# Entering the feed-forward steps: the second batch's A tiles in Bz buffers, their transfers ahead of later reads, and Bs asked for a unit earlier

## The chip, the cores and the metric

The kernel runs on one core of a Trainium2 chip. The metric is the device time of one execution in microseconds; the median of several executions counts. Beside it there is a profiled execution with its trace.

## The reference

Eight batches of 3008 x 256 (float32) go through a Fourier layer and then through a feed-forward network:

```python
X = np.fft.rfft(x, axis=1)
Yr = Xr @ w_r - Xi @ w_i + b_r;  Yi = Xr @ w_i + Xi @ w_r + b_i
Yr, Yi = soft_threshold(Yr, 0.01), soft_threshold(Yi, 0.01)
y = np.fft.irfft(Yr + 1j * Yi, n=3008, axis=1)          # -> 24064 x 256
h = y @ moe_w_in                                        # 256 -> 2048
g = np.where(h > 0, h, np.exp(np.minimum(h, 0)) - 1)    # ELU
out = g @ moe_w_out                                     # 2048 -> 256, float32
```

## The kernel before

**Fourier part, in units.** 3008 is split into 47 x 64, and each transform is two small matrix products with a trip through DRAM between them. A batch is worked in units: six A units (`unit_A`, first forward product from the x tiles `xt`; casts into an A tile, which is stored to the DRAM buffer DA), a load of Z from DA (`load_Z`, in two parts), eight X units (second forward product, into XT), twelve M half units (the complex weights, bias and soft threshold, into Y), six B units (`unit_B`, first inverse product, into a Bz tile, stored to the DRAM buffer DB), four loads of Bs from DB (`load_Bs`), and eight Y units (`unit_Y`, second inverse product, into yT). Two Y units share one Bs tile.

**Feed-forward part, in steps.** A step works one pair of 128-wide slices of the hidden dimension for 512 tokens: `front` multiplies yT with w_in_s into the PSUM tile hps and takes its exponential on ScalarE into Et; `elu` limits Et ("E" in the prediction); `finish_elu`, called in the next step, combines Et and hps into gT; and `back`, two steps behind (`LAG = 2`), multiplies gT with w_out_r into ps_o. Eight steps make a block of 512 tokens, after which ps_o is copied to osb and stored ("outs"). There are 47 steps to a batch. hps has two PSUM buffers, so step i+2 needs the gT of step i. A step without a unit is "free" and may take the exponential in halves and have GpSimd do the limiting.

**Order.** The order of the instructions on each engine is written out by hand. In the opening the first batch goes through all of its units alone; then come the second batch's six A units and the first batch's first two Y units, with matmuls on constants between them (`idle_pe(n)`, n matmuls whose result is dropped). From then on `plan` lays the units of the following batches over the steps, one to a step: `f0` runs before a step's `front`, `f1` after `finish_elu`. `lead` shifts the first batch's list by some steps.

**Queues.** Stores and most loads are issued by SyncE (SP), in program order; x and w_out are loaded from GpSimd's queue. w_out comes in two halves; the second holds the slices from ps_o 4 on, the fifth `back`. A `gate` is a copy of one element on GpSimd: it holds that queue back until a load has landed. w_in comes in four quarters, each scaled into w_in_s when it is there (`scale_w_in`); the last is scaled in two pieces on VectorE (DVE) in steps 3 and 4 and first used in step 6.

**Buffers.** Tiles with one tag share buffers in turn. The second batch's A tiles 1 and 2 lie in the buffers of the tag gT (three), which the steps then need.

The tail of the opening, as it is before:

```python
    for u in range(6):
        unit_A(1, u, on_dve=bool(u % 2), ahead=True)
        if u == 1:
            scale_w_in(1, True)
            for w in (2, 3):
                load_Bs(0, w)
            gate(Bs_of[0, 2][:, 0, 0:1])
            load_w_out(1)
            load_w_in(3)
        idle_pe(2)
    scale_w_in(2, False)
    for s0, s1 in ((0, 8), (8, NS)):
        load_Z(1, s0, s1)
    idle_pe(3)
```

Of the kernel before, what the change touches and what calls it, by code (L numbers as in the profile page):

```python
# [8 lines left out]
ALU = mybir.AluOpType  # L9
AF = mybir.ActivationFunctionType  # L10
BF16 = mybir.dt.bfloat16
# [18 lines left out]
def kernel(  # L30
# [11 lines left out]
    nc = tc.nc  # L42
    P = nc.NUM_PARTITIONS

    B, S, D = x.shape
# [33 lines left out]
    wk2 = ctx.enter_context(tc.tile_pool(name="wk2", bufs=2))  # L79
# [19 lines left out]
    A_of = {}  # L99
# [6 lines left out]
    Bs_of = {}  # L106
# [22 lines left out]
    def unit_A(b, u, alone=False, on_dve=False, ahead=False):  # L129
        ci, uu = u // 2, u % 2  # L130
        if uu == 0:
            if ahead and ci > 0:
                A_of[b, ci] = late3.tile([P, 8, D], BF16, name="A", tag="gT")
            elif alone:
                A_of[b, ci] = wk4.tile([P, 8, D], BF16, name="A", tag="Bs")
            else:
                A_of[b, ci] = wk2.tile([P, 8, D], BF16, name="A", tag="A")
            if ci == 0:
                DA_of[b] = dram.tile([NJ, P, D], BF16, name="DA", tag="DA")
        xt, A = xts[ci], A_of[b, ci]  # L140
        dav = DA_of[b].rearrange("j p d -> p j d")
        ps = unit_ps("aps", alone or ahead)
        for j in range(2):
            nc.tensor.matmul(  # L144
                ps[:, j, :], lhsT=M1[:],
                rhs=xt[:, 4 * uu + 2 * j : 4 * uu + 2 * j + 2, :], start=True, stop=True,
            )
        evac(
            A[:, 4 * uu : 4 * uu + 4, :].rearrange("p n d -> p (n d)"),
            ps[:].rearrange("p a b -> p (a b)"), on_dve,  # L150
        )
        j0 = 8 * ci
        if alone:
            j0 += 4 * uu
            nc.sync.dma_start(dav[:, j0 : j0 + 4, :], A[:, 4 * uu : 4 * uu + 4, :])
        elif uu == 1:
            nc.sync.dma_start(dav[:, j0 : j0 + 8, :], A[:])
# [109 lines left out]
    def load_Bs(b, w):  # L267

        Bs = wk4.tile([4 * K1, 8, D], BF16, name="Bs", tag="Bs")
        dv = DB_of[b].rearrange("k (c h m) d -> (k c h) m d", c=2, h=2)  # L270
        nc.sync.dma_start(Bs[:], dv[:, 8 * w : 8 * w + 8, :])
        Bs_of[b, w] = Bs

    def unit_Y(b, u, alone=False, on_dve=False):
        w, dt = u // 2, u % 2
        if u == 0:
            yT_of[b] = late2.tile([P, 2, S], BF16, name="yT", tag="yT")
        yT, Bs = yT_of[b], Bs_of[b, w]
        ps = unit_ps("yps", alone)
        psv = ps[:].rearrange("p a (k j) -> p (a k) j", j=P)  # L280
        for j in range(8):
            nc.tensor.matmul(  # L282
                psv[:, j, 0 : 2 * N1], lhsT=Bs[:, j, dt * P : dt * P + P], rhs=M4[:],
                start=True, stop=True,
            )
        evac(
            yT[:, dt, w * WT : w * WT + WT].rearrange("p (r j) -> p r j", j=8),
            psv[:, :, 0 : 2 * N1].rearrange("p j r -> p r j"), on_dve,
        )
# [5 lines left out]
    def idle_pe(n):  # L295

        for _ in range(n):
            nc.tensor.matmul(ips[:], lhsT=busy[:, 0:P], rhs=busy[:], start=True, stop=True)
# [274 lines left out]
    def load_w_in(q):  # L573
        if q < 3:
            wf = late3.tile([P, 2, FQ], F32, name="w_in_f", tag="Et")
        else:
            wf = late2.tile([P, 2, FQ], F32, name="w_in_f", tag="osb")
        nc.sync.dma_start(wf[:], w_in_v[:, :, q * FQ : q * FQ + FQ])
        w_in_f.append(wf)

    def load_w_out(hh):
        hf = slice(hh * NFT // 2, (hh + 1) * NFT // 2)
        nc.gpsimd.dma_start(w_out_r[:, hf, :], w_out_v[:, hf, :])

    def gate(src):

        t = gatep.tile([P, 1], F32, name="gate", tag="gate")
        nc.gpsimd.tensor_copy(t[0 : src.shape[0], :], src)
# [66 lines left out]
    def scale_w_in(q, on_dve, c=slice(0, 2)):  # L655
        dst = w_in_s[:, c, q * FQ : q * FQ + FQ]
        if on_dve:
            nc.vector.tensor_scalar_mul(dst, w_in_f[q][:, c], 2.0 / S)
        else:
            nc.scalar.activation(dst, w_in_f[q][:, c], AF.Copy, scale=2.0 / S)  # L660

    scale_w_in(0, True)
    for u in range(6):
        unit_A(1, u, on_dve=bool(u % 2), ahead=True)
        if u == 1:
            scale_w_in(1, True)
            for w in (2, 3):
                load_Bs(0, w)
            gate(Bs_of[0, 2][:, 0, 0:1])
            load_w_out(1)  # L670
            load_w_in(3)
        idle_pe(2)
    scale_w_in(2, False)
    for s0, s1 in ((0, 8), (8, NS)):
        load_Z(1, s0, s1)
    idle_pe(3)
    for u in range(2):
        unit_Y(0, u, alone=True, on_dve=bool(u % 2))
    first.close()

    psF = ctx.enter_context(
# [61 lines left out]
            g_of[i] = gT  # L743
        late_elu.clear()

    def elu(i, hps, Et, on_pool, on_act):

        E_ = Et[:]
        if on_pool:
            for s in range(2):  # L750
                eng = nc.vector if i == n - 1 and s == 0 else nc.gpsimd
                eng.tensor_scalar(E_[:, s], E_[:, s], 1.0, 0.0, ALU.min, ALU.max)  # L752
        elif not on_act:
            nc.vector.tensor_scalar(E_, E_, 1.0, -1.0, ALU.min, ALU.add)  # L754
        late_elu.append((i, hps, Et, on_pool or on_act, on_pool))

    def back(i, split):
        blk, fp = divmod(i, NPAIR)
# [41 lines left out]
    def plan(b):  # L800

        f0 = [[] for _ in range(PER)]
        f1 = [[] for _ in range(PER)]
        n1, n2 = b + 1, b + 2
        mid = [("X", u) for u in range(8)] + [
            ("M", 0, 0), ("M", 0, 1), ("M", 1, 0), ("M", 1, 1), ("B", 0), ("M", 2, 0),
            ("M", 2, 1), ("B", 1), ("M", 3, 0), ("M", 3, 1), ("B", 2), ("M", 4, 0),
            ("M", 4, 1), ("B", 3), ("M", 5, 0), ("M", 5, 1), ("B", 4),
            ("A", 0), ("B", 5), ("A", 1), ("A", 2), ("A", 3), ("A", 4),
        ]  # L810
        if n1 < B:
            lead, seq = int(b == 0), [("y", u) for u in range(2, 6)] + mid
            seq.insert(20 if b else 4, ("y", 6))
            seq.insert(24 if b else 5, ("y", 7))
            xs = (3, 8, 13)
            seq += [("A", 5), ("n", 0), ("n", 1)] if b else [("n", 0), ("n", 1), ("A", 5)]
        else:
            lead, seq = 0, [("y", u) for u in range(2, 8)]
        for t, u in enumerate(seq, lead):
            if u[0] == "y":  # L820
                f0[t].append(put("Y", b, u[1]))
            elif u[0] == "n":
                f0[t].append(put("Y", n1, u[1]))
            elif u[0] == "A":
                if n2 < B:
                    f0[t].append(put("A", n2, u[1]))
            else:
                f0[t].append(put(u[0], n1, *u[1:]))
            if u == ("A", 1):
                f1[t] += [(load_Bs, (n1, w)) for w in range(4)]  # L830
            if u == ("A", 5) and n2 < B:
                f1[t] += [(load_Z, (n2, s0, s1)) for s0, s1 in ((0, 8), (8, NS))]
        if b == 0:
            f1[3].append((scale_w_in, (3, True, 0)))
            f1[4].append((scale_w_in, (3, True, 1)))
            f1[xs[0]].append((lambda: gate(Z_of[1][:, 16, 0:1]), ()))
        if n2 < B:
            for ci in range(3):
                f1[xs[ci]].append((load_x, (n2, ci)))
        return f0, f1  # L840
# [3 lines left out]
    for i in range(n + LAG):  # L844
        if i < n:
            r = i % PER
            if r == 0:
                f0, f1 = plan(i // PER)
                used = [bool(u0 or u1) for u0, u1 in zip(f0, f1)]
            free = not used[r]  # L850
            bare = bare + 1 if free else 0
            calm = free and (i >= n - 2 or (r + 2 < PER and not used[r + 1] and not used[r + 2]))
            for f, a in f0[r]:
                f(*a)
            on_act = any(f is unit_M for f, a in f0[r])
            h = front(i, calm and bare % 3 == 1, on_act, free and i > 0)
        finish_elu()
        if i < n:
            for f, a in f1[r]:
                f(*a)  # L860
            split = i > LAG and (i - LAG) % NPAIR == NPAIR - 1
            if split:
                back(i - LAG, True)
            elu(i, *h, free and i > 0, on_act)
        else:
            split = False
        if i >= LAG and not split:
            back(i - LAG, False)
# [30 lines left out]
```

## Time and profile before

| what | value |
|---|---|
| median of 3 runs | 912.44 us (912.34 to 914.53) |
| profiled execution | 911.36 us, its span 909.6 us |
| granted TensorE clock over the span | 0.997 |
| TensorE (PE) busy | 893.2 us, 98% |
| VectorE (DVE) busy | 717.5 us, 79% |
| ScalarE (ACT) busy | 696.8 us, 77% |
| GpSimd (POOL) busy | 314.9 us, 35% |
| DMA | 106.24 MB, mean 117 GB/s |

The span runs from the first to the last instruction of the program; the execution's time is 1.8 us longer. Times inside the trace count from the span's start. PE is the matmuls, PEld the weight loads beside them; SPq is SyncE's queue of DMA issues. A number in brackets behind a row is the idle time of the engine before it and what ended it.

### The profile page before, as it was taken

To read this page: it belongs to the slowest core of one execution; us is meant where nothing else is said; L and a number is where in the kernel's file an instruction comes from. 1 tells how busy PE (TensorE), PEld (TensorE's weight loads), DVE (VectorE), ACT (ScalarE), POOL (GpSimd) and SP (SyncE) were. 2 spreads that over 40 slices of the span, in tenths; PEclk is the share of its full clock that TensorE was granted. 3 is DMA by queue.
4 is the path that set the end of the run, shared out by engine and by line. 5 is a ranking of instruction groups with operands and counts; after the bars stand their busy time and mean duration, and the time that the engine had idled before them with its cause. 6 is when DMAs were issued, how large, how long until landed. Compare 5 with 4: busy or idle time off the path is not lost.

```text
span 909.6 us, 17270 instructions
## 1 busy us (share of the span) xinstructions
PE 893.2 (98%) x6721; PEld 652.3 (72%) x6721; DVE 717.5 (79%) x891; ACT 696.8 (77%) x850; POOL 314.9 (35%) x438
## 2 busy tenths in 40 slices
PE   8989999999999999999999999999999999999997
PEld 3447667876688667886678766787667866777775
DVE  8669778887788778897788877888778877778776
ACT  6768788777878778787787888778887877767664
POOL 6701540333321441405404153033332134443664
PEclk9999999999999999999999999999999999999999
DMA  8997116721283215732166032752228111231011
GB/s 270 309 269 228 47 48 186 209 70 47 77 241 124 71 47 143 190 109 85 56 201 194 24 99 59 217 161 72 69 72 230 30 42 47 82 82 48 24 48 46
DMA packets 90670, 106.24 MB, mean 117 GB/s; under 512 B 5270, under 2 KB 81308, under 8 KB 87228
## 3 DMA queue, kind: packets, MB, share of 16 engines
q1 hardware_dynamic: 84332, 77.62, 30.6%
q0 software_dynamic: 5968, 27.26, 9.1%
q8 instruction: 52, 0.85, 0.4%
q10 hardware_dynamic: 288, 0.26, 0.1%
q14 instruction: 30, 0.25, 0.1%
HBM read 55.32 MB, written 49.81 MB: 116 GB/s over the span
## 4 chain that ended last, share of the span: by engine, by line
PE 85%; DVE 5%; ACT 3%; DMA 3%; issue 2%; POOL 1%; SPq 1%; DVEq 0%; ACTq 0%; POOLq 0%
PE ps_o L773 34%; PE hps L715 34%; PE mps L192 9%; PE yps L282 2%; PE bps L244 2%; PE xps L175 2%; PE aps L144 2%; DMA Bs<-DB 2%; DVE gT L742 1%; DVE Et L754 1%; ACT Et L729 1%; ACT Et L726 1%; DMA xt<-in_x_dram 1%; DVE osb L784 1%; ACT Bz L257 1%
## 5 line engine op out<-in xcount | busy, mean ns | idle before, releaser
L773 PE MATMUL ps_o<-w_out_r,gT 128*128 128x256 f32 x3008 | 477.0, 301 | 0.2 <-DVE gT L740 0.2
L773 PEld LDWEIGHTS ps_o<-w_out_r,gT 128*128 128x128 f32 x3008 | 403.4, 189 | 50.3 <-DVE osb L784 1.3
L715 PE MATMUL hps<-yT,w_in_s 128*128 128x512 bf16 (+4 forms) x1728 | 389.9, 353 | 2.5 <-DVE gT L742 1.2
L740 DVE SCALAR_TENSOR_TENSOR gT<-Et,hps 128x512 fp32r<-128x512 f32 (+1 forms) x272 | 222.8, 848 | 75.3 <-POOL Et L752 38.2
L742 DVE SCALAR_TENSOR_TENSOR gT<-hps,Et 128x1024 fp32r<-128x1024 f32 x198 | 242.2, 1223 | 16.5 <-PE ps_o L773 1.0
L715 PEld LDWEIGHTS <-w_in_s 128*128 128x128 bf16 x1728 | 141.6, 98 | 129.4 <-issue 23.0
L729 ACT ACTIVATE Et<-hps 128x1024 f32<-128x1024 f32 x198 | 204.0, 1030 | 13.2 <-PE hps L715 6.7
L752 POOL TENSOR_SCALAR Et<-Et 128x512 f32<-128x512 f32 x187 | 111.4, 615 | 222.9 <-ACT Et L724 222.9
L754 DVE TENSOR_SCALAR Et<-Et 128x1024 f32<-128x1024 f32 x198 | 137.0, 692 | 48.0 <-ACT Et L729 40.1
L210 POOL TENSOR_SCALAR clip<-yb 128x512 f32<-128x512 f32 x84 | 51.7, 615 | 316.0 <-DVE yb L202 278.6
L724 ACT ACTIVATE Et<-hps 128x512 f32<-128x512 f32 x188 | 102.1, 595 | 63.9 <-PE hps L715 63.9
L726 ACT ACTIVATE Et<-hps 128x1024 f32<-128x1024 f32 x84 | 86.3, 1027 | 71.5 <-PE hps L715 71.0
L211 POOL TENSOR_TENSOR Y<-yb,clip 128x512 bf16<-128x512 f32 x84 | 107.2, 1276 | 7.0
L727 ACT ACTIVATE Et<-Et 128x1024 f32<-128x1024 f32 x84 | 88.8, 1058 | 2.7
L202 DVE TENSOR_TENSOR yb<-mps,bias_bc 128x512 f32<-128x512 f32 x89 | 61.4, 689 | 35.4 <-PE mps L192 28.6
L127 ACT CAST XT<-xps 128x768 bf16<-128x768 f32 x61 | 48.8, 800 | 15.8 <-PE xps L175 15.8
L127 ACT CAST yT<-yps 128x752 bf16<-128x752 f32 x63 | 49.7, 788 | 14.2 <-PE yps L282 14.1
L192 PE MATMUL mps<-wcat_r,XT 128*128 128x512 bf16 x192 | 58.2, 384 | 0.8 <-ACT Bz L257 0.3
L127 ACT CAST A<-aps 128x1024 bf16<-128x1024 f32 x45 | 45.6, 1014 | 15.3 <-PE aps L144 13.8
L192 PE MATMUL mps<-wcat_s,XT 128*128 128x512 bf16 x192 | 57.1, 379 | 0.0
L192 PEld LDWEIGHTS <-XT 128*128 128x128 bf16 x384 | 30.8, 98 | 29.6 <-DVE XT L125 0.6
L257 ACT CAST Bz<-bps 128x1024 bf16<-128x1024 f32 x46 | 46.0, 1000 | 2.5 <-PE bps L244 2.5
(110 smaller groups left out, 412.9 us busy)
## 6 DMA issues: line engine op xcount, KB each, us to landing
xt<-in_x_dram POOLq DMA_DIRECT2D x21, 1024.0 KB, 7.1
out_dram<-osb SPq DMA_DIRECT2D x158, 128.0 KB
Bs<-DB SPq DMA_DIRECT2D x32, 384.0 KB
DA<-A SPq DMA_DIRECT2D x21, 512.0 KB
DB<-Bz SPq DMA_DIRECT2D x21, 512.0 KB
Z<-DA SPq DMA_DIRECT2D x7, 1152.0 KB
Z<-DA SPq DMA_DIRECT2D x11, 384.0 KB
xt<-in_x_dram POOLq DMA_DIRECT2D x6, 512.0 KB, 5.9
```

The lines of the kernel that those rows point to most:

```text
L127: nc.scalar.copy(dst, src)
L192: nc.tensor.matmul(ps, lhsT=XT[:, dt, c, o : o + P], rhs=wm[:, dt, :], start=(not biased and m == 0 and dt == 0), stop=(m == 1 and dt == 1),)
L211: nc.gpsimd.tensor_tensor(Y_of[b, q][:, i, :], yb, clip[:], ALU.subtract)
L715: nc.tensor.matmul(hps[:, s, c0:c1], lhsT=w_in_s[:, dt, ft * P : ft * P + P], rhs=yT_of[b][:, dt, t0 : t0 + c1 - c0], start=(dt == 0), sto ...
L724: nc.scalar.activation(E_[:, s], hps[:, s], AF.Exp)
L726: nc.scalar.activation(E_, hps[:], AF.Relu, scale=-1.0)
L729: nc.scalar.activation(E_, hps[:], AF.Exp)
L740: nc.vector.scalar_tensor_tensor(o, e, -1.0, h, ALU.add, ALU.max)
L742: nc.vector.scalar_tensor_tensor(o, h, 0.0, e, ALU.max, ALU.add)
L752: eng.tensor_scalar(E_[:, s], E_[:, s], 1.0, 0.0, ALU.min, ALU.max)
L754: nc.vector.tensor_scalar(E_, E_, 1.0, -1.0, ALU.min, ALU.add)
L773: nc.tensor.matmul(po[q][:, i_ % 2, :], lhsT=gT[:, s, i_ * P : i_ * P + P], rhs=w_out_r[:, ft, :], start=(ft == 0 and i_ % 2 == 0), stop=( ...
```

## The change

Six edits. In the opening, the second batch's A tiles 1 and 2 are given the buffers of the tag Bz. The loads of the first batch's last two Bs tiles, the gate, the second half of w_out and the last quarter of w_in are issued after all six A units, and so behind all three stores to DA, instead of after the second. The idle matmuls ahead of the first two Y units become seven instead of three, and two are added behind them. In the steps, the first batch's list begins at step 2 instead of 1. Steps 0 and 1, both free now, take the exponential, the limiting and the combining in halves, on ScalarE and VectorE. In every batch the four Bs tiles are asked for in the step of the last B unit instead of that of the second A unit, which comes one step later.

```diff
             if ahead and ci > 0:
-                A_of[b, ci] = late3.tile([P, 8, D], BF16, name="A", tag="gT")
+                A_of[b, ci] = wk2.tile([P, 8, D], BF16, name="Bz", tag="Bz")
...
         if u == 1:
             scale_w_in(1, True)
-            for w in (2, 3):
-                load_Bs(0, w)
-            gate(Bs_of[0, 2][:, 0, 0:1])
-            load_w_out(1)
-            load_w_in(3)
         idle_pe(2)
     scale_w_in(2, False)
+    for w in (2, 3):
+        load_Bs(0, w)
+    gate(Bs_of[0, 2][:, 0, 0:1])
+    load_w_out(1)
+    load_w_in(3)
     for s0, s1 in ((0, 8), (8, NS)):
         load_Z(1, s0, s1)
-    idle_pe(3)
+    idle_pe(7)
     for u in range(2):
         unit_Y(0, u, alone=True, on_dve=bool(u % 2))
+    idle_pe(2)
     first.close()
...
-    def elu(i, hps, Et, on_pool, on_act):
+    def elu(i, hps, Et, on_pool, on_act, halves):
...
         elif not on_act:
-            nc.vector.tensor_scalar(E_, E_, 1.0, -1.0, ALU.min, ALU.add)
-        late_elu.append((i, hps, Et, on_pool or on_act, on_pool))
+            for s in range(2) if halves else (slice(0, 2),):
+                nc.vector.tensor_scalar(E_[:, s], E_[:, s], 1.0, -1.0, ALU.min, ALU.add)
+        late_elu.append((i, hps, Et, on_pool or on_act, halves))
...
-            lead, seq = int(b == 0), [("y", u) for u in range(2, 6)] + mid
+            lead, seq = 2 * int(b == 0), [("y", u) for u in range(2, 6)] + mid
...
-            if u == ("A", 1):
+            if u == ("B", 5):
                 f1[t] += [(load_Bs, (n1, w)) for w in range(4)]
...
-            h = front(i, calm and bare % 3 == 1, on_act, free and i > 0)
+            h = front(i, calm and bare % 3 == 1, on_act, free)
...
-            elu(i, *h, free and i > 0, on_act)
+            elu(i, *h, free and i > 1, on_act, free)
```

## The prediction

> **What bounds the kernel now.** The page comes first. TensorE is busy for 98% of the span, so what a change can win or lose lies in TensorE's idle time and in matmuls at a lowered clock.
>
> ```profile
> span 909.6 us, 17270 instructions
> PE 893.2 (98%) x6721; PEld 652.3 (72%) x6721; DVE 717.5 (79%) x891; ACT 696.8 (77%) x850; POOL 314.9 (35%) x438
> ```
>
> The timeline of TensorE alone, 54 to 74 us, shows where the edited lines run: the entry from the opening into the feed-forward steps. "Step i" is iteration i of the main loop; hps i, gT i and ps_o i are its two products and what lies between.
>
> ```profile
> 55.16 0.84 PE L282 MATMUL yps<-M,Bs 96*128 96x94 bf16 x16 [1.01 <-DMA Bs<-DB]
> 56.54 1.55 PE L715 MATMUL hps<-yT,w_in_s 128*128 128x512 bf16 x4 [0.54 <-ACT yT L127]
> 58.51 1.91 PE L715 MATMUL hps<-yT,w_in_s 128*128 128x512 bf16 x4
> 64.53 1.02 PE L715 MATMUL hps<-yT,w_in_s 128*128 128x512 bf16 x4 [0.96 <-DVE gT L742]
> 71.65 1.28 PE L773 MATMUL ps_o<-w_out_r,gT 128*128 128x256 f32 x8
> ```
>
> The brackets are the idle time before a row. hps 1 takes 1.91 us where the settled form takes 1.02. The last row, at 71.65, is ps_o 4, the first to read the second half of w_out. Two other timelines (DVE, and POOL) show what stands before it:
>
> ```profile
> 63.25 1.23 DVE L742 SCALAR_TENSOR_TENSOR gT<-hps,Et 128x1024 fp32r<-128x1024 f32 x1 [1.04 <-PE ps_o L773]
> 59.37 0.55 POOL L588 CAST gate<-Bs 96x1 f32<-96x1 bf16 x1 [15.26 <-DMA Bs<-DB]
> 59.87 0.97 POOL L583 DMA_DIRECT2D w_out_r<-in_moe_w_out_dram  x1
> ```
>
> gT 1 waits 1.04 us for ps_o 0, since the A tiles hold two of the three gT buffers. The gate waits for the third Bs tile and only then is w_out asked for; the tile view of w_out_r gives 9.6 us from issue to landing, so it lands at 69.45: 2.2 us ahead of ps_o 4. The SyncE queue and the windows view (us in the window, busy times of PE, PEld, DVE, ACT, POOL, then granted clock, DMA share, GB/s):
>
> ```profile
> 52.47 1.54 SPq L271 DMA_DIRECT2D Bs<-DB  x2
> 54.05 1.55 SPq L578 DMA_DIRECT2D w_in_f<-in_moe_w_in_dram  x1
> 55.70 1.64 SPq L157 DMA_DIRECT2D DA<-A  x2
> 66.83 0.82 SPq L164 DMA_DIRECT2D Z<-DA  x2
> 61.00:66.00 5.00, 3.80 (x31) 2.86 (x30) 3.62 (x5) 3.38 (x5) 0.00 (x0) 1.00 1.23 345
> 66.00:74.00 8.00, 8.00 (x78) 6.31 (x77) 7.45 (x11) 6.74 (x8) 0.00 (x0) 1.00 1.03 262
> 74.00:77.00 3.00, 3.00 (x29) 2.58 (x27) 2.76 (x3) 2.62 (x4) 1.57 (x3) 1.00 0.00 0
> 54.04:57.45 3.41, 1.75 (x20) 1.03 (x20) 1.22 (x2) 0.79 (x1) 0.00 (x0) 1.00 1.05 323
> 57.45:60.87 3.42, 3.42 (x22) 2.01 (x21) 1.58 (x2) 2.11 (x3) 1.47 (x2) 0.50 1.03 267
> ```
>
> From 52 to 74 us the DMA engines never pause, and at 74 they fall to nothing: a solid train of 6.3 MB (four Bs 1.57 MB, three DA 1.57, w_in 0.52, w_out 1.05, Z 1.57). In such a train an order is a deadline. And a 3.41 us stretch in which TensorE was busy for 1.75 us was followed by one at half clock.
>
> Last, the chain of waits around the second batch's first Y unit:
>
> ```profile
> 143.24 6.07 DMA Bs<-DB
> 149.31 0.05 issue
> 149.35 0.51 PE yps L282 x8
> ```
>
> TensorE stands 0.91 us there, and 1.03 us at 796.8 in the last batch. Beyond 66 us those are its only gaps over 0.2 us.
>
> **The change part by part.** *Idle matmuls.* Six more at 0.216 us (five took 1.25 us, the last draining) are 1.3 us. Four lie in the 1.01 us wait for Bs, two in the 0.54 us wait for yT. Cost nothing; without that cover 1.3. They keep 54.04 to 57.45 busy, so hps 0 and 1 run at full clock.
>
> *Bz buffers, halves, Y a step later.* The Bz tiles' reads were asked for by 44.95 and the DMA engines were at 0 GB/s from 51 to 52, so the new A tiles wait for nothing (cost 0; a wait would show on the casts of 50 to 54 us). I redo the steps from their durations: hps 0.86 issued, ps_o 0.93, a Y unit 0.35, a whole exp 1.03, E 0.69, gT 1.23 (1.14 to the next start), halves 0.6, 0.4, 0.66. hps 0 is issued by 57.7 (it waits for yT until 57.03 as before), halved exps end at 59.0, gT 0 at 60.75 (before 61.21). hps 1 and Y 2 run to 58.9, then TensorE waits. hps 2 60.8 to 61.65, ps_o 0 to 62.6, Y 3 to 62.95; gT 1 has its own buffer and ends by 62.7; hps 3 to 63.8, ps_o 1 to 64.75, Y 4 to 65.1, hps 4 to 65.95, ps_o 2 and Y 5 to 67.25.
>
> *The train.* Bs 2 and 3, the gate, w_out's second half and w_in's last quarter move behind two DA transfers: 2 x 0.524 MB at 345 GB/s is 3.04 us. The gate goes from 59.37 to 62.4, w_out's issue to 62.9. Bs 2 lands at 62.3, before Y 4 at 64.75. w_in's last packet was at 61.5 by the packet records, so 64.5, landed near 65.5; DVE's scaling at step 3, in front of E 3, would be ready at 64.9 and waits 0.6 us. gT 3 then ends at 67.9, hps 5 to 68.8, ps_o 3 and Y 6 to 70.1, hps 6 (after gT 4 at 70.2) to 71.1. There ps_o 4 wants w_out. Before, the same point was 72.0 (71.65 is its early start) with Y 7 done, 0.35 us: with w_out in time the entry is 72.0 - 71.1 - 0.35 = 0.55 us shorter.
>
> w_out is not in time. Z waits for the last DA; that DA's packets now end at 60.1 (57.07 + 3.04), and before Z was issued 0.5 us after them: so at 60.7, ahead of w_out at 62.9. The bytes are the same, the train ends at 74.0 as before, but its last car is w_out where it was Z. From last packet to landing w_out took 0.95 us (68.5 to 69.45), and its last packets straggle: 75.2. ps_o 4 starts at 75.2 instead of 72.0, one Y unit behind: 3.2 + 0.35 = **+3.55 us**. Bounds: 69.7 (served on arrival: 1.1 us to the first packet, as the x load at 75.93, then 5.7 as before) and 76.0 (1 us of straggling).
>
> Why last: in the packet records a newcomer waits for what another queue already holds. The out stores issued at 80.04 send nothing until x's packets thin out at 84; the DB store issued at 36.82 nothing until 39.25, when w_out's first half thins out; w_out itself, issued at 59.87, nothing until 63.75. The Trainium skill, "DMA: Bandwidth & Descriptors", section on queues, rings and completion order, has each DMA engine go round robin between queues packet by packet; by equal turns w_out would pass Z, which is the first rival below. The trace shows such turns only from 64 to 65 us (about 50 packets each per quarter), after the wait.
>
> *Clock.* TensorE then idles from 71.1 to 75.2. A stretch busy for 1.75 of 3.41 us halved the next, so nearly wherever the stretches fall one follows. Half clock after the restart costs half of what is left of it: 0.85 to 2.5, I take **+1.5**. The Trainium skill, "TensorE: Matmul & The Clock Gate", Part 1, gives the slow state after at least one idle window of about 3.4 us; a 4.1 us gap holds a whole one in one phase of five, so by the page this term would mostly be 0 and the time 915.1. The row speaks for less idleness being enough.
>
> *Bs asked for earlier.* SyncE waits for the DB store to land; queued behind are A's stores, which nobody needs before Z is asked for. In the first batch outs now come just before that store, as they do in the last batch. From the start of B 5's matmuls: SP is done with four outs at 3.3 us (the outs of 139.87 began 0.6 into their step and took 2.6), DB lands 3.5 us later (789.86 to 793.35), Bs 4.4 after that (793.41 to 797.8): 11.2. The Y unit comes at 11.6 (136.87 to 148.44). So the gap of 0.91 goes: **-0.9**; with the last batch's own 12.85 (784.93 to 797.78) it would grow by 0.4, the other bound. In the last batch SP reaches Bs the moment DB lands (793.41), earlier asking moves nothing: 0. Other batches have no gap: 0.
>
> Sum: 3.55 + 1.5 - 0.9 = +4.2. The profiled execution took 911.36 (span 909.6 and 1.8 around it), 1.1 below the median; it becomes 915.5, the median 916.6.
>
> **The rivals.** *Queues share* (15%): w_out takes turns with Z as it did with the DA stores and lands 9.6 us after its issue again, 72.5: 72.5 - 72.0 + 0.35 = +0.85, clock 0.4 for the shorter idling, Bs -0.9, so +0.35: 912.8. For it the even turns of 64 to 65 us; against it the three late starts. *w_out first* (13%, the other side): GpSimd's queue served on arrival, landed 69.7, no stall: -0.55 - 0.9 = -1.45: 911.0. It decides when w_out lands before 71.1. For it x's full rate over outs at 81 to 84; against it that x was there first. *All in time* (12%): w_in lands by 64.9 too, so gT 3 ends 0.6 us earlier, and the last batch's gap goes as well, 1.0: -1.45 - 0.6 - 1.0 = -3.05: 909.4. It needs the DA stores at 430 GB/s (0.6 of 3.04 us less; they ran at 345) and a Bs load that does not wait for DB.
>
> **How the numbers follow.** Forecast 60%; its own range, from landing (-1.2, +0.8), clock and Bs, 914.2 to 919.2. To leave out no more than two in ten the range reaches down through w_out first: 910.8 to 919.2. A measurement of this kernel tells 0.3% from no change, 2.7 us. Slower beyond that: the forecast less its lowest twentieth, 0.57. Within: that twentieth and the two middle rivals, 0.31. Faster: all in time, 0.12.
>
> **What would show it.** In the changed trace: the gate near 62.4, w_out's landing near 75, an idle time of some 4 us before ps_o 4 put down to the w_out DMA, a clock of 0.50 behind it, clock 1.00 at 57 to 60, no gap at the second batch's first Y unit, the gap near 797 + 5 still there. Wrong if ps_o 4 starts at once near 71, or if Z's packets end after w_out's.

## The result, and the profile after

The changed kernel takes 967.64 us (median of 6, 965.47 to 968.97) where the kernel before takes 912.4 (6 runs). The ratio is 1.0601, 95% interval 1.0585 to 1.0617: slower by 55 us, where 4 had been forecast. The first lines of the page show what kind of loss it is.

```profile
span 963.7 us, 17180 instructions
PE 905.0 (94%) x6623; PEld 663.1 (69%) x6727; DVE 718.4 (75%) x895; ACT 698.0 (72%) x852; POOL 314.6 (33%) x438
```

The span grew by 54.1 us and TensorE's busy time by 11.8 only (somewhat too little, since this trace holds 98 matmul records fewer): most of the loss is idleness, and part is matmuls that take longer. Which idleness is told by one group of the page, the casts of the A tiles on ScalarE (before, then after; behind the second bar the idle time ahead of them and what ended it):

```profile
L127 ACT CAST A<-aps 128x1024 bf16<-128x1024 f32 x45 | 45.6, 1014 | 15.3 <-PE aps L144 13.8 <-ACT Et L729 1.4
```
```profile
L127 ACT CAST A<-aps 128x1024 bf16<-128x1024 f32 x43 | 43.6, 1013 | 47.8 <-DMA DA<-A 35.6 <-PE aps L144 12.0
```

A wait of 35.6 us for a store, DA<-A, which did not exist before; the view of waits has it as six waits, the longest 7.3 us. The timeline shows the second of the six, in the fourth batch's A units (SPq: SyncE issuing; the Bs are the third batch's), with the same place one batch earlier in the kernel before:

```profile
263.48 0.36 SPq L265 DMA_DIRECT2D DB<-Bz  x1
264.78 1.01 ACT L127 CAST A<-aps 128x1024 bf16<-128x1024 f32 x1 [0.35 <-PE aps L144]
266.74 2.74 SPq L271 DMA_DIRECT2D Bs<-DB  x4
269.57 0.38 SPq L157 DMA_DIRECT2D DA<-A  x1
276.67 1.01 ACT L127 CAST A<-aps 128x1024 bf16<-128x1024 f32 x1 [5.36 <-DMA DA<-A]
277.74 0.97 PE L144 MATMUL aps<-xt,M 128*128 128x512 f32 x2 [4.41 <-ACT A L127]
```
```profile
142.52 0.55 SPq L157 DMA_DIRECT2D DA<-A  x1
143.24 2.72 SPq L271 DMA_DIRECT2D Bs<-DB  x4
146.72 1.01 ACT L127 CAST A<-aps 128x1024 bf16<-128x1024 f32 x1 [0.36 <-PE aps L144]
```

The row at 264.78 is the cast of A 1. It ends at 265.79 and its tile is ready to be stored, but SyncE stands before the Bs loads until the DB store has landed, and issues them (from 266.74 on) first. The store goes out at 269.57, behind 1.57 MB of Bs. A 4 writes the third A tile of the batch; the tag A has two buffers, so that tile is the first one's, and its cast stands until the store has landed. Before, the store was asked for ahead of Bs and the cast waited for nothing but its matmul. TensorE has six such gaps (6.3, 4.4, 4.2, 5.7, 4.4 and 5.0 us, sum 30.0), and behind each a stretch at half clock; half of the busy time in those stretches is 13.9 us, which is what they cost. Together 43.9 of the 54.1. At the first of the six the chain of waits, which before ran through the Bs load there, runs through the A store:

```profile
151.64 3.48 DMA DB<-Bz
157.01 7.76 DMA DA<-A
166.72 1.71 PE hps L716 x4
```

The opening went nearly as forecast (timelines of TensorE, POOL and SyncE; this execution reached it some 1.25 us later: Bs landed at 56.35, before at 55.1):

```profile
61.92 1.02 PE L716 MATMUL hps<-yT,w_in_s 128*128 128x512 bf16 x4 [1.63 <-DVE gT L743]
69.87 1.02 PE L716 MATMUL hps<-yT,w_in_s 128*128 128x512 bf16 x4 [1.35 <-DVE gT L743]
77.53 2.07 PE L775 MATMUL ps_o<-w_out_r,gT 128*128 128x256 f32 x8 [4.37 <-DMA w_out_r<-in_moe_w_out_dram]
```
```profile
64.20 1.10 POOL L583 DMA_DIRECT2D w_out_r<-in_moe_w_out_dram  x1
```
```profile
62.25 0.78 SPq L164 DMA_DIRECT2D Z<-DA  x2
```

Z is asked for ahead of w_out, w_out lands last (77.49), and ps_o 4 stands 4.37 us for it. The windows behind it (us; PE, PEld, DVE, ACT, POOL; clock, DMA share, GB/s):

```profile
76.66:80.07 3.41, 2.54 (x17) 2.45 (x18) 0.00 (x0) 0.00 (x0) 1.58 (x3) 0.50 0.72 214
80.07:83.49 3.42, 3.20 (x15) 2.41 (x13) 0.43 (x1) 1.81 (x2) 0.00 (x0) 0.50 1.06 424
83.49:86.90 3.41, 3.41 (x34) 2.60 (x34) 2.32 (x4) 2.55 (x3) 0.00 (x0) 1.00 0.74 291
```

Two windows at half clock (0.50), not one.

### The profile page after: what moved, and what is told of

Its sections match the earlier page's. It is cut to its first block, busy times and chain, and to the rows that moved or that the text cites. A ratio compares the mean times of both kernels' runs of the same rounds, so it can differ in the third digit from the quotient of the medians.

```text
span 963.7 us, 17180 instructions
## 1 busy us (share of the span) xinstructions
PE 905.0 (94%) x6623; PEld 663.1 (69%) x6727; DVE 718.4 (75%) x895; ACT 698.0 (72%) x852; POOL 314.6 (33%) x438
## 4 chain that ended last, share of the span: by engine, by line
PE 79%; DMA 9%; DVE 4%; ACT 4%; issue 2%; POOL 1%; SPq 1%; ACTq 0%; DVEq 0%; POOLq 0%
PE ps_o L775 31%; PE hps L716 31%; PE mps L192 8%; DMA DA<-A 5%; PE bps L244 2%; PE yps L282 2%; PE aps L144 2%; PE xps L175 2%; DMA w_out_r<-in_moe_w_out_dram 1%; DVE gT L743 1%; DMA Bs<-DB 1%; DVE Et L756 1%; ACT Et L730 1%; ACT A L127 1%; DMA xt<-in_x_dram 1%
## 5 line engine op out<-in xcount | busy, mean ns | idle before, releaser
L775 PE MATMUL ps_o<-w_out_r,gT 128*128 128x256 f32 x3008 | 484.3, 304 | 4.6 <-DMA w_out_r<-in_moe_w_out_dram 4.4
L775 PEld LDWEIGHTS ps_o<-w_out_r,gT 128*128 128x128 f32 x3008 | 409.9, 191 | 56.4 <-DMA w_out_r<-in_moe_w_out_dram 4.9
L716 PE MATMUL hps<-yT,w_in_s 128*128 128x512 bf16 (+7 forms) x1655 | 389.3, 356 | 9.3 <-DVE gT L743 3.0
L743 DVE SCALAR_TENSOR_TENSOR gT<-hps,Et 128x1024 fp32r<-128x1024 f32 (+1 forms) x200 | 242.3, 1212 | 16.4 <-PE hps L716 1.4
L756 DVE TENSOR_SCALAR Et<-Et 128x1024 f32<-128x1024 f32 (+1 forms) x200 | 137.2, 686 | 97.3 <-ACT Et L730 88.9
L725 ACT ACTIVATE Et<-hps 128x512 f32<-128x512 f32 x192 | 104.2, 596 | 65.4 <-PE hps L716 63.3
L127 ACT CAST A<-aps 128x1024 bf16<-128x1024 f32 x43 | 43.6, 1013 | 47.8 <-DMA DA<-A 35.6
L144 PE MATMUL aps<-xt,M 128*128 128x512 f32 x96 | 34.1, 439 | 26.0 <-ACT A L127 23.7
L192 PE MATMUL mps<-wcat_s,XT 128*128 128x512 bf16 x182 | 54.9, 379 | 0.9
L192 PE MATMUL mps<-wcat_r,XT 128*128 128x512 bf16 x175 | 54.5, 384 | 1.0 <-ACT Bz L257 0.5
```

The lines of the kernel that those rows point to most:

```text
L127: nc.scalar.copy(dst, src)
L192: nc.tensor.matmul(ps, lhsT=XT[:, dt, c, o : o + P], rhs=wm[:, dt, :], start=(not biased and m == 0 and dt == 0), stop=(m == 1 and dt == 1),)
L716: nc.tensor.matmul(hps[:, s, c0:c1], lhsT=w_in_s[:, dt, ft * P : ft * P + P], rhs=yT_of[b][:, dt, t0 : t0 + c1 - c0], start=(dt == 0), sto ...
L725: nc.scalar.activation(E_[:, s], hps[:, s], AF.Exp)
L743: nc.vector.scalar_tensor_tensor(o, h, 0.0, e, ALU.max, ALU.add)
L756: nc.vector.tensor_scalar(E_[:, s], E_[:, s], 1.0, -1.0, ALU.min, ALU.add)
```

## The experiments

The theory after the comparison: the Bs edit makes the first A store of a batch late on SyncE's queue, and through the shared buffer that stops TensorE (some 44 us); the moved loads cost what the opening shows. The rivals are given with each run.

**bs_undone and bs_only: each half of the change alone.** The first is the changed kernel with the old place of the Bs loads, the second the kernel before with nothing but the new place.

```diff
-            if u == ("B", 5):
+            if u == ("A", 1):
```

> The change with one edit undone: the four Bs tiles are asked for in the step of the second A unit again. Buffer theory (the cast of a batch's third A tile waits for the store of the first, which SyncE now issues behind four Bs loads that wait for DB): the six gaps of 4.2 to 6.3 us and the half clock behind them go, 30.0 + 18.8 us: about 919 us. Opening theory (the order of the opening's loads makes the loss): over 950. Clock theory (gaps stay, only fewer): between.

> The kernel before with only the Bs edit. Buffer theory: before plus 48.8, less at most 0.9 for the gap at the second batch's first Y unit: 960 to 961. Opening theory: 912 within 1.

Measured beside 912.47: bs_undone 920.38, ratio 1.0088 (1.0069 to 1.0106); bs_only 954.02, 1.0451 (1.0427 to 1.0474). The Bs edit alone makes 41.6 us of the loss. Its trace has the six gaps (5.0, 4.6, 4.3, 4.6, 4.3, 5.1, sum 27.8), and half of the busy time at half clock behind them is 14.1 us. Of the 7 us by which I expected too much, 2.2 are gaps shorter than the changed kernel's 30.0; the rest is the expectation's 18.8, which is half of the whole stretches at half clock (37.5 us) and counts TensorE's idle time in them a second time. bs_undone has none of the six, but it has the gap at ps_o 4 (4.51) with 6.83 us of half clock.

**third_A: is it the buffer?** The changed kernel, with a buffer of its own for the third A tile from the third batch on.

```diff
+            elif b > 1 and ci == 2:
+                A_of[b, ci] = a3p.tile([P, 8, D], BF16, name="A", tag="A3")
+    a3p = ctx.enter_context(tc.tile_pool(name="a3p", bufs=1))
```

> The change with a third buffer for a batch's third A tile, from the third batch on; SyncE's order and all transfers as in the change. Buffer theory: the waits of the casts go although the first A store is as late as in the change: 918, some 0.9 under bs_undone if the gap at the second batch's first Y unit is gone. Transfer theory (the Bs loads ahead of the A stores crowd the DMA engines, and something needs the late data whatever the buffers): over 950.

Measured 919.87, 1.0074 (1.0056 to 1.0093). SyncE does the same things in the same order, the A store still goes out behind Bs, and the cast of A 4 (263.78) no longer waits for it:

```profile
258.89 2.56 SPq L273 DMA_DIRECT2D Bs<-DB  x4
261.54 0.38 SPq L159 DMA_DIRECT2D DA<-A  x1
263.78 1.01 ACT L127 CAST A<-aps 128x1024 bf16<-128x1024 f32 x1 [0.26 <-PE aps L146]
```

**act_store: is it the place in SyncE's queue?** bs_only, with that one store issued from ScalarE's queue; the buffers stay shared.

```diff
-            nc.sync.dma_start(dav[:, j0 : j0 + 8, :], A[:])
+            q = nc.scalar if b > 1 and ci == 0 else nc.sync
+            q.dma_start(dav[:, j0 : j0 + 8, :], A[:])
```

> The kernel before with the Bs edit alone (954.0), and the first A store of each batch from the third on (the one whose buffer A 4 needs) issued on ScalarE's own DMA queue instead of SyncE's. Bs and the store's bytes, buffers and order of work stay as they are; only the place in SyncE's queue goes. If the place in the queue is the cause, the store is issued at the end of A 1's cast, about 0.8 us ahead of the first Bs read, its packets share with little, it lands before A 4's cast is due: no gaps of 4 us, 911.5 to 914 (an issue on ScalarE costs it perhaps 0.1 to 0.7 us in six steps). Rival, that the bytes of Bs and outs hold the store up wherever it is issued: gaps of 2 us and more stay, above 930.

Measured 913.65 beside 912.51, 1.0017 (1.0007 to 1.0026). The store (ACTq: ScalarE issuing) is issued at 249.5, ahead of the first Bs load, and A 4's cast waits only for its matmul:

```profile
L158 ACTq DMA_DIRECT2D DA<-A x1: 366/366/366, 249.5 to 249.5; - x1
```
```profile
250.35 2.24 SPq L272 DMA_DIRECT2D Bs<-DB  x4
```
```profile
255.51 1.01 ACT L127 CAST A<-aps 128x1024 bf16<-128x1024 f32 x1 [0.35 <-PE aps L144]
```

So it takes both, the place in the queue and the shared buffer; removing either removes the loss. What remains fits the issue on ScalarE, 0.37 us: laid step by step over the kernel before, this trace slips by 0.27 to 0.36 us at the step of A 1 in each of the six batches.

**hold, bs_w0 and bs_eighth: which part of the late issue costs?** In bs_only the cast waits 5.5 us. I had put it down to SyncE standing for DB (1.4), four issues (2.7) and the bytes of Bs ahead (3.0), less 1.8 of slack. hold keeps only the first; bs_w0 asks early for one of the four Bs tiles.

```diff
+            if u == ("B", 5):
+                f1[t].append((touch_DB, (n1,)))      # hold: 96 x 2 elements of DB
```
```diff
+            if u == ("B", 5):
+                f1[t].append((load_Bs, (n1, 0)))     # bs_w0; w = 1 to 3 stay in A 1's step
```

> The kernel before, with one read of two columns of DB (96 partitions x 4 bytes) put on SyncE's queue in B 5's step, where the changed kernel asks for Bs; Bs itself is asked for in A 1's step as before. So SyncE is held until the DB store lands, but no Bs byte and almost no issue stands ahead of the first A store. My decomposition of the 5.5 us by which A 4's cast waits (third batch of the run with the Bs edit alone): SyncE held for DB 1.4, four Bs issues 2.7, Bs bytes ahead in the DMA engines 3.0, less 1.8 us of slack that the order of before had. Hold alone is 1.4 (perhaps 1.9 with the small read's own issue) against 1.8 of slack: no gap over 0.5 us at A 4, 912 to 913.5. Rival, that holding the queue is the whole of it and the bytes merely follow: gaps of 3 us and more before the A 4 matmuls and half clock behind them, above 935.

> The kernel before, with only the first of the four Bs reads asked for in B 5's step and the other three in A 1's as before. Ahead of the first A store then stand the hold (1.4 us), one issue (0.7) and a quarter of the bytes (0.75): 2.85 less 1.8 of slack = some 1 us of wait at A 4's cast in six batches, too short to bring half clock (gaps of 0.9 us did not before). 912 + 6 x 1.0 = 918 if all of it reaches TensorE, 913 if the hold and the bytes overlap (the bytes are moved while SyncE issues). I take 914. Rival, that any reading of DB ahead of the store costs the whole: near 954.

hold: 920.74, 1.0095 (1.008 to 1.0111). The part that it was made for came out: SyncE stands until 254.83, the store goes out at once behind, and no A 4 in any batch costs TensorE a gap.

```profile
254.83 0.33 SPq L277 DMA_DIRECT2D touch<-DB  x1
255.26 0.38 SPq L157 DMA_DIRECT2D DA<-A  x1
255.73 3.15 SPq L271 DMA_DIRECT2D Bs<-DB  x4
259.87 1.01 ACT L127 CAST A<-aps 128x1024 bf16<-128x1024 f32 x1 [0.36 <-PE aps L144]
```

The total missed by 7 us: Bs comes too late for the second batch's first Y unit (a gap of 3.17 for 0.91, and 3.41 us of half clock behind it, all busy, which cost 1.7), and about 4 us are spread thinly over the batches behind it. In the free steps at the end, which touch neither DB nor Bs, the mean ps_o matmul takes 305 ns for 301. Why stays open; it wasn't tried apart.

bs_w0: 919.63, 1.0083 (1.0069 to 1.0098), worse than the 914 that I took. The gaps at A 4 are there, small: step by step against the kernel before, it slips by 0.8, 0.6, 0.9, 0.8 and 1.8 us in the five later batches, and in the first of the six 1.45 us stand where 0.91 for Bs stood; none brings half clock. So holding SyncE is within the slack, one Bs tile ahead of the store then costs about 1 us, and four of them about 4.6 and the half clock. How much of it is the issues and how much the bytes stays open. The rival that any early read costs the whole is refuted.

bs_eighth was to cut the bytes: bs_only with an eighth of each Bs tile read from the second batch on and the rest set to zero by GpSimd, so that those batches work on partial data.

```diff
+        if k < 8:
+            nc.gpsimd.memset(Bs[:, k:8, :], 0.0)
-        nc.sync.dma_start(Bs[:], dv[:, 8 * w : 8 * w + 8, :])
+        nc.sync.dma_start(Bs[:, 0:k, :], dv[:, 8 * w : 8 * w + k, :])
```

> bs_only with an eighth of the bytes in the Bs loads from the second batch on (the rest of each tile is set to zero by GpSimd, so those batches' Y units work on partial data); number, order and waits of SyncE's issues as in bs_only. What makes the first A store late: if SyncE's order alone (held until DB lands, then four issues), the gaps of 4.3 to 5.1 us stay and the time is over 945. If the 1.57 MB that the A store queues behind on the DMA engines alone, the gaps go: 912 within 1.5. If both, gaps of 1 to 3 us and 920 to 940.

Measured 945.65 beside 911.82, 1.0364 (1.034 to 1.0388), and it tells nothing about bytes. The cast waits are gone, but the filling is a new wait:

```profile
243.66 6.18 POOL L273 MEMSET Bs<- 96x1792 bf16 x4
245.74 4.66 DVE L757 TENSOR_SCALAR Et<-Et 128x1024 f32<-128x1024 f32 x1 [0.61 <-ACT Et L732]
251.78 1.86 PE L718 MATMUL hps<-yT,w_in_s 128*128 128x512 bf16 x4 [3.84 <-DVE gT L745]
```

DVE's limiting of Et, 0.69 us elsewhere, takes 4.66 while GpSimd fills, hps stands 3.84 us for gT, and in that stall SyncE catches up. The experiment was badly made.

**bs_third: is early Bs worth what I said, once it costs nothing?** bs_only with third_A's buffer.

> The kernel before with the Bs edit alone, and a buffer of its own for the third A tile of each batch, so that A 4 waits for no store. This is the Bs edit without its cost, and so tests the -0.9 us that I gave it: the gap of 0.91 us at the second batch's first Y unit goes, that of 1.03 in the last batch shrinks to 0.4 to 0.6 as in the changed kernel: 0.9 + 0.5 = 1.4 less than before, 910.5 to 911.2. Rival, that the late stores now make Z late for the X units in some batch: gaps before xps put down to the Z load, 912.5 or more.

Measured 911.38 beside 912.51, 0.9988 (0.9979 to 0.9997). The gap of 0.91 at the second batch's first Y unit is gone; that of the last batch is 1.55 here for 1.03:

```profile
149.08 0.51 PE L284 MATMUL yps<-M,Bs 96*128 96x94 bf16 x8
```
```profile
798.04 0.51 PE L284 MATMUL yps<-M,Bs 96*128 96x94 bf16 x8 [1.55 <-DMA Bs<-DB]
```

Step by step against the kernel before, this trace gains 1.1 us at the first place and loses 0.5 at the last. The loss can't be put down to the edit: in the traces with Bs asked for early and no cast waiting the last gap is 0.41 (best), 0.77 (act_store), 0.78 (third_A) and 1.55, and in those with Bs as before it runs from 0.34 (bs_undone) to 1.03. In all of these Bs is asked for 3.5 to 3.9 us after the DB store; what differs is the time from there to the Y unit, 3.7 to 4.9 us. So only the first gap tells of the edit.

**loads_early: what do the moved loads cost?** bs_undone, with Bs 2 and 3, the gate, w_out and w_in back where they were, behind the second A unit of the opening.

> The change with two edits undone: Bs as before, and in the opening the last two Bs loads, the gate, the second half of w_out and the last quarter of w_in issued after the second A unit as before. What is left: Bz buffers, idle matmuls, halves in steps 0 and 1, the list a step later. The prediction's step (entry 0.55 us shorter with w_out in time): 911.9, ps_o 4 without a wait. Rival (the list a step later and halves cost time of themselves): over 913.5. Against bs_undone this gives the price of the moved loads: predicted 4 to 6 us.

Measured 911.68 beside 912.47, 0.9993 (0.9983 to 1.0003): what is left of the change is worth nothing measurable, and the moved loads cost 920.38 - 911.68 = 8.7 us, more than the 4 to 6 expected. A gap that I had not foreseen stands at the second batch:

```profile
153.36 1.00 PE L716 MATMUL hps<-yT,w_in_s 128*128 128x64 bf16 x7 [0.84 <-ACT yT L127]
```

With the list a step later Bs has a step more to land, and its gap of 0.91 is gone without the Bs edit; but the second Y unit now falls in the step whose hps needs its yT, and waits 0.84: one gap took the other's place.

**gate_Bs1: is w_out late because it is asked for last?** bs_undone, the gate on the second Bs tile in place of the third.

```diff
-    gate(Bs_of[0, 2][:, 0, 0:1])
+    gate(Bs_of[0, 1][:, 0, 0:1])
```

> bs_undone with the gate on the second Bs tile instead of the third; SyncE's order as in the change. GpSimd asks for w_out some 5 us earlier, ahead of Z. Train theory (what is asked for first goes first): w_out lands near 70, ps_o 4 does not wait, no half clock behind it; what stays is the wait of step 3 for w_in, 1.3 us: 912.5 to 914. Rival (the two DA stores ahead of the reads are what delays w_out, wherever it is asked for): ps_o 4 still waits over 2 us, 916 or more.

Measured 920.96 beside 911.82, 1.0098 (1.0078 to 1.0118): no gain, which is the rival's time, but by another wait than either side had. w_out is asked for at 56.14, some 7 us earlier than in the changed kernel with the starts matched (Bs is asked for at 56.34 here, 57.57 there), and lands at 76.90. Its first packets go at 59.4, up to 207 in a microsecond while SyncE's queue has little (61 to 62); once Bs and w_in come, w_out sends 58 to 63 packets of 1 KB per us beside 57 to 62 of SyncE's queue (from 63 to 66 us, mostly 4 KB and 2 KB each). The last 52 of its 1024 packets take from 70 to 76.4, beside Z's packets of 12 KB. So w_in is now the late one: VectorE stands 6.68 us for it, hps 5 stands 5.42 us for the gT that VectorE makes only then, and ps_o 4, at 78.95, finds w_out there.

```profile
71.17 0.43 DVE L658 TENSOR_SCALAR w_in_s<-w_in_f 128x512 bf16<-128x512 f32 x1 [6.68 <-DMA w_in_f<-in_moe_w_in_dram]
```

**lead1 and best: what is the change good for?** lead1 is loads_early with the first batch's list shifted by one step again; best adds third_A's buffer and the Bs edit.

```diff
-            lead, seq = 2 * int(b == 0), [("y", u) for u in range(2, 6)] + mid
+            lead, seq = int(b == 0), [("y", u) for u in range(2, 6)] + mid
```

> loads_early with the first batch's list beginning at step 1 again. The wait of the batch's last front for the second Y unit's yT (0.84 us) goes, since that unit is a step earlier; the wait for hps 2 is filled by a Y unit (0.35); the gap for Bs at the second batch's first Y unit (0.91) may come back: 910.5 without it, 911.4 with it. Rival (a step of room for Bs is worth more): over 912.

> lead1 with the third A buffer and Bs asked for in the last B unit's step. If the third buffer takes the harm out of the early Bs, the gap at the second batch's first Y unit stays away and the last batch's shrinks: 910.2, below before by more than its scatter. If early Bs loads still cost (late A stores, late Z), 912 or more.

lead1: 911.59 beside 911.82, 0.9997 (0.9987 to 1.0006): the yT gap goes and 0.58 for Bs comes back. best: 909.93, 0.9978 (0.9969 to 0.9987), ahead of both kernels. Its own next bound is in the opening: X 0 is reached before Z has landed.

```profile
73.06 0.51 PE L177 MATMUL xps<-M,Z 96*128 96x96 bf16 x8 [1.23 <-DMA Z<-DA]
```

## Why the prediction was wrong

**The step that failed** is the sentence under *Bs asked for earlier*: "queued behind are A's stores, which nobody needs before Z is asked for". I named what is queued behind the waiting instruction and asked who reads the data, but not who needs the buffer. A 4's cast does: three A tiles in two buffers. "Other batches have no gap: 0" rests on the same sentence; at six places, one to a batch, TensorE lost 30.0 us idle and 13.9 at half clock. "No gap at the second batch's first Y unit", one of the signs named, failed for this reason: 6.3 us stand there. No rival held it either, so the range ended at 919.2. Shown by third_A and act_store.

**The benefit of that edit was right for the edit alone.** -0.9 with bounds of -0.9 and +0.4 for the second batch's gap: bs_third has it gone, 1.1 us less in the medians. That the last batch's Bs is asked for no earlier was right too (3.5 us behind the DB store in both). In the change itself the term is luck: the Y list, a step later, removes that gap alone and puts 0.84 in its place (loads_early), and third_A, with the Bs edit, stands 0.5 under bs_undone, without it, which their intervals don't tell apart.

**The stall at ps_o 4 was right.** Forecast: gate 62.4, w_out issued 62.9, landed 75.2. Measured less the 1.25 of the late start: 62.8, 62.95, 76.2, a gap of 4.37 for 4.1. The hps 2 wait is there (1.63), and w_in made DVE wait 1.3 us rather than 0.6, seen at hps 5 as 1.35. Steps 0 and 1 ran at full clock, as forecast: without the idle matmuls three of seven traces have a window at half clock there (before, bs_only, act_store), with them none of seven.

**The clock term was too small.** +1.5 with bounds of 0.85 and 2.5; the half clock lasted 6.83 us, of which 5.74 busy: 2.9. I had halved one window only; the window in which TensorE restarts (busy 2.54 of 3.41) brought another. The Trainium skill, "TensorE: Matmul & The Clock Gate", Part 1, asks for a whole idle window; here a window of 1.75 busy (before) and one of 1.04 (ahead of 161.99) were followed by half clock, so the row was the better guide, and not yet enough.

**Part of the opening was missed.** The change without the Bs edit (bs_undone) stands 7.9 us above the kernel before, against my 3.55 + 1.5 = 5.05; or, from loads_early, 8.7 for the moved loads against 5.6, since 0.55 of gain stood on the other side. The clock term is 1.4 of the difference, the landing about 1.0. The rest was not taken apart. The three bounds, added up, give 914.75 to 919.7 where the text has 914.2 to 919.2; neither holds the result.

**"A newcomer waits for what another queue already holds" was half of it.** In the changed kernel w_out sent nothing from its issue at 64.2 until 70.6, as said. gate_Bs1 shows what follows such a wait: turns packet by packet, which is what the Trainium skill, "DMA: Bandwidth & Descriptors", section on queues, rings and completion order, states; the counts from 63 to 66 us agree. But equal turns do not bring the *queues share* rival: they are turns of packets, 1 KB of w_out against 2 or 4 KB beside it, so w_out moves 58 to 63 KB in a microsecond there, and lands at 76.90 even when it is asked for 7 us sooner. Beside Z, from 70 to 75 us, the counts are no longer equal (4 to 14 a microsecond against 16 to 27); why w_out's last packets straggle was not taken apart.

## What to carry to other kernels

When a waiting instruction is moved up a queue, list every transfer behind it and ask two questions of each: who reads what it writes, and who is to write into the buffer that it reads. Count the tiles that are alive against the buffers of their tag in the steady state, since a wait of 5 us that recurs in every batch, with the half clock behind it, outweighs all that this opening could win. And moving one transfer ahead in this full train only chose which one was late: w_out, or w_in (gate_Bs1).

## What the runs showed of the hardware

**The clock follows windows of 3.41 us on a fixed grid, and a full stop is not needed.** In each trace all stretches at half clock begin and end whole multiples of 3.413 us apart, but for the end of the last, behind the program's end. With that grid laid over all fourteen traces from 50 us on: of the windows at full clock, all 22 in which TensorE was busy for 1.16 us or less were followed by half clock, none with 1.86 or more was, and between 1.5 and 1.81 it went either way. A window already at half clock needs more to get out: with up to 2.38 us busy the next was at half clock again (11 of 11), with 3.18 and more never, mixed between. So gaps of 4.2 to 4.6 us were followed by one such window in some batches and by two in others, as they lay on the grid; the second is seen in the changed kernel's windows at 387 to 397 us, where a busy 2.23 of 3.41 did not restore the clock.

```profile
387.28:390.69 3.41, 0.41 (x4) 0.22 (x2) 0.59 (x1) 0.00 (x0) 0.00 (x0) 1.00 1.08 308
390.69:394.10 3.41, 2.23 (x5) 0.98 (x6) 1.22 (x2) 2.91 (x3) 0.00 (x0) 0.50 0.70 231
394.10:397.51 3.41, 3.41 (x20) 2.86 (x19) 2.18 (x3) 1.36 (x3) 0.00 (x0) 0.50 0.51 159
```

**A GpSimd fill can hold VectorE up:** in bs_eighth an operation of 0.69 us took 4.66 beside four fills of 96 x 1792, and 4.65 to 4.86 in five of the seven batches with such fills.
